# A 4 MB zero fill at the end of a kernel, changed from an SBUF store into a DRAM-to-DRAM copy with an outer dimension of 15

## The chip, the cores and the metric

The kernel runs on one core of one Trainium2 chip. The metric is the device time of one execution in microseconds, as the median of several.

## The reference

The reference computes one decode step of a small transformer block (attention over the last 4096 of 32768 cached positions, then a gated layer) and all gradients. What matters here is the size of two of the outputs: the gradients of the K cache and of the V cache.

```python
Hq, Dh = 16, 256
Hkv, Sk = k_cache.shape[1], k_cache.shape[2]          # 8, 32768
W = min(4096, max(256, Sk // 4))                      # 4096
k = jnp.repeat(k_cache[:, :, Sk - W:, :], rep, axis=1)
v = jnp.repeat(v_cache[:, :, Sk - W:, :], rep, axis=1)
...                                                   # scores, softmax, output, gated layer
_out, _vjp = jax.vjp(_f, A_x, A_k_cache, A_v_cache, A_wq, A_wo, B_w_gate, B_w_up, B_w_down)
```

Each cache gradient has 8 x 32768 x 256 bf16 elements, 128 MiB. Only the last 4096 positions of each head are not zero. So seven eighths of both outputs, 224 MiB, are zeros that somebody has to write.

## The kernel before

The zeros come from a zeroed part of SBUF (`arena`). The POOL queue writes most of them throughout the kernel. A few fills of 4 MB and 2 MB, the "late jobs", go on the SP queue behind the last computed results.

```python
ZW = 8192
def zero_rows(o, g, n0, n1, f):
    reg = o[0, g, 0:Sk - W, :].rearrange("s d -> (s d)")[n0 * 128 * ZW:n1 * 128 * ZW]
    return reg.rearrange("(n p f) -> n p f", p=128, f=f)

late_jobs = [(out_2, G - 1, 5, 7, 2 * ZW), (out_3, G - 1, 0, 6, 2 * ZW), (out_3, G - 1, 6, 7, ZW)]
...
def send_fills(n0, n1, halves=False):                  # the POOL queue
    for reg in fills[n0:n1]:
        ...
        ZQ.dma_start(out=reg, in_=zeros)
...
for it, g in enumerate(order):                         # the eight heads of the backward pass
    ...
    for o_ap, st_ in ((out_3, stV), (out_2, stK)):
        LD.dma_start(out=o_ap[0, g, Sk - W:, :].rearrange("(p t) d -> p t d", t=T), in_=st_)
    ...
for o, g, n0, n1, f in late_jobs:                      # the SP queue
    reg = zero_rows(o, g, n0, n1, f)
    for i in range(reg.shape[0]):
        LD.dma_start(out=reg[i], in_=ar(2 * ZW - f, f))
```

The last stores on the SP queue are, in this order: four of 2 MB (results), then the late fills of 4 MB, 4 MB and 2 MB. The change is about the second of the two 4 MB fills.

## Time and profile before

| what | value | from |
|---|---|---|
| time | 802.11 us (801.46 to 802.81) | three executions |
| DMA busy | 9 tenths or more in 39 of 40 slices | slices of the page |
| moved | 334.84 MB, mean 418 GB/s | slices of the page |
| last work of PE, DVE, ACT | before 720 us | windows |
| end of the slowest DMA engine | 799.0 us | packet records |

These lines are from the page of the kernel before: the span, the slices of the DMA engines, and the queues (packets, bytes, and the share of the time of 16 engines).

```profile
span 800.5 us, 8486 instructions
...
DMA  9999999999999999999999999999999999999994
GB/s 350 431 430 429 428 430 430 427 428 428 431 426 422 428 417 409 420 422 428 433 423 425 424 430 428 429 426 426 424 427 423 426 420 425 423 424 427 423 440 192
...
q0 software_dynamic: 16496, 216.01, 63.8%
q1 hardware_dynamic: 11382, 116.68, 34.7%
...
q8 instruction: 25, 0.41, 0.2%
...
HBM read 53.69 MB, written 280.59 MB: 418 GB/s over the span
```

The DMA row says that the engines are busy from start to end; q0 is the POOL queue, q1 the SP queue. So the span is bytes divided by rate, except for the last slice, whose DMA share falls to 4 tenths. The next view is the table by windows of the kernel before. Its columns are the window, its length, busy time and instructions of PE, PEld, DVE, ACT and POOL, the granted clock, the mean busy share of the 16 DMA engines, and GB/s.

```profile
720.00:740.00 20.00, 0.00 (x0) 0.00 (x0) 0.00 (x0) 0.00 (x0) 0.00 (x0) 0.50 1.03 429
...
775.00:780.00 5.00, 0.00 (x0) 0.00 (x0) 0.00 (x0) 0.00 (x0) 0.00 (x0) 0.50 0.99 426
780.00:785.00 5.00, 0.00 (x0) 0.00 (x0) 0.00 (x0) 0.00 (x0) 0.00 (x0) 0.50 0.97 416
785.00:790.00 5.00, 0.00 (x0) 0.00 (x0) 0.00 (x0) 0.00 (x0) 0.00 (x0) 0.50 0.74 315
790.00:795.00 5.00, 0.00 (x0) 0.00 (x0) 0.00 (x0) 0.00 (x0) 0.00 (x0) 0.50 0.18 75
795.00:800.50 5.50, 0.00 (x0) 0.00 (x0) 0.00 (x0) 0.00 (x0) 0.00 (x0) 0.50 0.04 18
```

No compute engine works after 720 us. The share 0.04 is below one engine in sixteen (0.0625): at the end a single DMA engine is working. The view of the waits of the SP queue says the same from the other side (columns: who waited for whom, total us, times, longest us). Line 683 is the end of the program:

```profile
SPq L683 <- DMA out_dram<-arena: 52.7, 4, 28.6
```

The chain of waits is of no help here. Its last piece is an end-of-program step of DVE at 719 us, because it does not follow the draining stores.

The packet records of the trace tell more. A record has a start, a length, a size and a queue, but no engine. In this trace 99.7% of the packets of 16 KB and more that end between 470 and 560 us have another packet's start within 6 ns of their end, so records can be chained. From 460 us on I did this with a search that also respects the order of both queues; it is a reconstruction, and where two engines run in step it could swap them. In the tail it is unambiguous. The last packets of the engine that ends last, which I call A (start us, length ns, bytes; all on the SP queue):

```
784.438  1213  32768    first of eight 32 KB packets of the second 4 MB fill
...                     one every 1210 ns
792.904  1213  32768
794.113     9      4    closes the fill
794.119   611  16384    first of eight 16 KB packets of the last 2 MB fill
...                     one every 607 ns
798.369   611  16384
798.976     9      4    closes the fill, the end
```

The trace has 2820 packets of 4 bytes and 2822 semaphore updates by DMA. The 103 transfers of the POOL queue have 1648 of these packets, 16 each, so I count one per transfer and engine.

Fourteen engines end between 786.0 and 791.5 us, one (B) at 795.3, and A at 799.0.

### The profile page before, as it was taken

Reading aid. Unit: us, or ns where it says so; the run is one execution under the profiler, and the core shown is the slowest. Engines: PE = TensorE matmul, PEld = TensorE weight load, DVE = VectorE, ACT = ScalarE, POOL = GpSimd, SP = SyncE. Lnnn points to the kernel's source line nnn. Section 1 sums busy time; section 2 is a strip of 40 time slices with the busy share of each in tenths; the row PEclk is TensorE's granted clock in tenths of the full one; section 3 lists DMA queues with packets and bytes.
Section 4 is the critical chain, followed back from the end, with each engine's and each line's share of the span. In section 5 each row is a group of like instructions: output and inputs, shape, how many; then the busy total and the mean of one; then the engine's idle time right before and its main releaser. Section 6 shows DMA issues by size and latency. Waiting matters only on the chain.

```text
span 800.5 us, 8486 instructions
## 1 busy us (share of the span) xinstructions
PE 459.3 (57%) x3182; PEld 245.9 (31%) x3182; DVE 370.2 (46%) x1176; ACT 196.3 (25%) x309; POOL 62.0 (8%) x112
## 2 busy tenths in 40 slices
PE   0459999999999994623239295845262064520000
PEld 0334554545545552312129143322021022200000
DVE  2115363472552652255770975766681187660000
ACT  0143313224133100000002054643241045340000
POOL 4000000010100110101100010000000000000000
PEclk9978999999999997555559699776557567655555
DMA  9999999999999999999999999999999999999994
GB/s 350 431 430 429 428 430 430 427 428 428 431 426 422 428 417 409 420 422 428 433 423 425 424 430 428 429 426 426 424 427 423 426 420 425 423 424 427 423 440 192
DMA packets 29359, 334.84 MB, mean 418 GB/s; under 512 B 2819, under 2 KB 5894, under 8 KB 7814
## 3 DMA queue, kind: packets, MB, share of 16 engines
q0 software_dynamic: 16496, 216.01, 63.8%
q1 hardware_dynamic: 11382, 116.68, 34.7%
q10 hardware_dynamic: 1440, 1.61, 0.6%
q8 instruction: 25, 0.41, 0.2%
q14 instruction: 16, 0.13, 0.0%
HBM read 53.69 MB, written 280.59 MB: 418 GB/s over the span
## 4 chain that ended last, share of the span: by engine, by line
PE 35%; DMA 33%; DVE 15%; ACT 4%; issue 2%; another core or an unknown queue 0%; SPq 0%; ACTq 0%; DVEq 0%
DMA out_dram<-arena 19%; PE M_ps L311 11%; PE ok_ps L315 6%; PE rows_ps L255 6%; PE tr_ps L252 4%; DMA dh_bc<-in_grad_out_dram 4%; DMA arena<-in_A_k_cache_dram 4%; ACT arena L269 2%; DMA arena<-in_A_wo_dram 2%; DVE arena L645 2%; DVE arena L454 2%; DVE arena L646 2%; DMA arena<-in_B_w_up_dram 2%; PE dqb_ps L497 2%; DMA arena<-in_B_w_gate_dram 2%; DVE arena L509 2%
## 5 line engine op out<-in xcount | busy, mean ns | idle before, releaser
L307 DVE TENSOR_SCALAR arena<-arena,p_f 128x256 bf16<-128x256 bf16 x512 | 109.8, 280 | 67.0 <-PE M_ps L311 67.0
L311 PE MATMUL M_ps<-arena 128*128 128x512 bf16 x512 | 122.9, 381 | 0.0
L255 PE MATMUL rows_ps<-arena,vpad 128*16 128x512 bf16 x256 | 85.9, 431 | 22.2 <-DVE arena L608 16.9
L252 PE MATMUL tr_ps<-ident_bf,arena 128*128 128x128 bf16 x1024 | 87.9, 236 | 15.0 <-DMA arena<-in_A_k_cache_dram 8.4
L132 POOL DMA_DIRECT2D out_dram<-arena x90 | 48.8, 544 | 560.7 <-DMA out_dram<-arena 522.7
L252 PEld LDWEIGHTS <-arena 128*128 128x128 bf16 x1024 | 65.9, 105 | 65.0 <-issue 55.4
L638 PE MATMUL d_ps<-arena,rT 32*128 32x512 bf16 x256 | 43.6, 511 | 69.6 <-DVE arena L646 50.2
L269 ACT COPY arena<-tr_ps 128x1024 bf16<-128x1024 bf16 x64 | 61.7, 1015 | 87.9 <-PE tr_ps L252 87.9
L311 PEld LDWEIGHTS <-arena 128*128 128x128 bf16 x512 | 46.2, 99 | 50.8 <-issue 6.5
L315 PE MATMUL ok_ps<-arena 128*16 128x256 bf16 x512 | 57.5, 273 | 0.9 <-DVE arena L296 0.9
L606 ACT COPY arena<-tr_ps 128x1024 bf16<-128x1024 bf16 x32 | 32.5, 1016 | 96.1 <-PE tr_ps L252 39.3
L642 ACT CAST arena<-d_ps 128x512 bf16<-128x512 f32 x64 | 37.6, 588 | 71.5 <-PE d_ps L638 71.5
L645 DVE CAST arena<-d_ps 128x512 bf16<-128x512 f32 x64 | 43.9, 686 | 14.9 <-PE d_ps L638 14.6
L315 PEld LDWEIGHTS <-arena 128*16 128x16 bf16 x512 | 45.4, 90 | 13.9 <-issue 3.4
L646 DVE CAST arena<-d_ps 128x512 bf16<-128x512 f32 x64 | 43.5, 680 | 8.3 <-DMA out_dram<-arena 8.3
L638 PEld LDWEIGHTS <-rT 32*128 32x128 bf16 x256 | 11.2, 95 | 95.4 <-issue 52.1
L643 ACT CAST arena<-d_ps 128x512 bf16<-128x512 f32 x64 | 38.0, 594 | 9.1 <-DMA out_dram<-arena 9.1
L255 PEld LDWEIGHTS <-vpad 128*16 128x16 bf16 x256 | 18.9, 91 | 57.1 <-issue 49.3
L318 ACT COPY arena<-M_ps 128x512 f32<-128x512 f32 x16 | 8.6, 589 | 75.0 <-PE M_ps L311 75.0
L509 DVE CUSTOM_DVE_ANT_0 arena<-arena 128x4096 bf16<-128x4096 bf16 x3 | 13.1, 4422 | 23.1 <-ACT arena L502 23.1
L608 DVE COPY arena<-tr_ps 128x1024 bf16<-128x1024 bf16 x32 | 21.7, 680 | 4.1 <-PE tr_ps L252 4.0
L631 DVE TENSOR_SCALAR arena<-R_sb,tl_f 128x512 bf16<-128x512 bf16 x64 | 17.8, 347 | 2.1 <-ACT R_sb L628 1.9
(198 smaller groups left out, 358.1 us busy)
## 6 DMA issues: line engine op xcount, KB each, us to landing
out_dram<-arena POOLq DMA_DIRECT2D x103, 2048.0 KB, 53.5
out_dram<-arena SPq DMA_DIRECT2D x18, 2048.0 KB, 32.7
arena<-in_A_v_cache_dram SPq DMA_DIRECT2D x10, 2048.0 KB, 49.6
arena<-in_A_k_cache_dram SPq DMA_DIRECT2D x8, 2048.0 KB, 29.7
out_dram<-arena SPq DMA_DIRECT2D x4, 4096.0 KB, 57.2
arena<-in_A_wq_dram SPq DMA_DIRECT2D x2, 3072.0 KB, 20.5
arena<-in_A_wo_dram SPq DMA_DIRECT2D x2, 1792.0 KB, 16.2
out_dram<-arena SPq DMA_DIRECT2D x2, 1792.0 KB, 33.2
```

The lines of the kernel that those rows point to most:

```text
L132: ZQ.dma_start(out=reg, in_=zeros)
L252: nc.tensor.transpose(tr_ps[:, dh, i, :], X_sb[:, 4 * q + i, dh * 128:(dh + 1) * 128], ident_bf[:])
L255: nc.tensor.matmul(rows_ps[:], lhsT=pad[:, dh, 16 * q:16 * q + 16], rhs=XT[:, dh].rearrange("p t k -> p (t k)"), start=(q == 0 and dh == 0 ...
L269: sT_ps = dots(kv_at(K_off[g]), KT_slot, vpad[g % 2], rows1, ps_c, "cols", lambda q, XT, ps: nc.scalar.copy(out=XT, in_=ps))
L307: nc.vector.tensor_scalar(out=pK[:, i, hh, :], in0=K_sb[:, t, :], scalar1=p_f[:, 8 * i + c, hh:hh + 1], scalar2=None, op0=ALU.mult)
L311: nc.tensor.matmul(M_ps[:, vh, :], lhsT=V_sb[:, t, vh * 128:(vh + 1) * 128], rhs=pK[:, i, :, :].rearrange("p h d -> p (h d)"), start=(t == ...
L315: nc.tensor.matmul(ok_ps[:, k, :], lhsT=ppad[g % 2][:, 8 * (t % 4) + t // 4, :], rhs=X_sb[:, t, :], start=(g == 0 and k == 0 and t == 0), ...
L638: nc.tensor.matmul(d_ps[:, qi].rearrange("p w d -> p (w d)"), lhsT=rT[32 * q:32 * (q + 1), :], rhs=RB_[32 * q:32 * (q + 1), l, :], start=T ...
L642: nc.scalar.copy(out=stV[:, t:t + 2, :], in_=d_ps[:, :, 0, :])
L643: nc.scalar.copy(out=stK[:, t:t + 2, :], in_=d_ps[:, :, 1, :])
L645: nc.vector.tensor_copy(out=stV[:, t:t + 2, :], in_=d_ps[:, :, 0, :])
L646: nc.vector.tensor_copy(out=stK[:, t:t + 2, :], in_=d_ps[:, :, 1, :])
```

## The change

The intent is to take one fill off the engine that ends last. The copy has an outer dimension of 15, to leave one of the sixteen engines out; if that one is the late one, it is spared 9.7 us. The source is a region of the K gradient that was zeroed hundreds of microseconds earlier.

```diff
+        done = zero_rows(out_2, 0, 0, 2, 2 * ZW)[0].rearrange("p f -> (p f)")
+
+        def fifteen(flat):
+            return flat[0:15 * 17 * ZW].rearrange("(a b) -> a b", b=17 * ZW)
+
         for o, g, n0, n1, f in late_jobs:
             reg = zero_rows(o, g, n0, n1, f)
             for i in range(reg.shape[0]):
-                LD.dma_start(out=reg[i], in_=ar(2 * ZW - f, f))
+                if (n0, i) == (0, 2):
+                    with tc.issue_after(getattr(last, "ins", last)):
+                        flat = reg[i].rearrange("p f -> (p f)")
+                        for lo, hi in ((0, 16 * ZW), (16 * ZW, 17 * ZW)):
+                            LD.dma_start(out=fifteen(flat)[:, lo:hi], in_=fifteen(done)[:, lo:hi])
+                        LD.dma_start(out=flat[255 * ZW:256 * ZW].rearrange("(o f) -> o f", o=1), in_=done[255 * ZW:256 * ZW].rearrange("(o f) -> o f", o=1))
+                else:
+                    last = LD.dma_start(out=reg[i], in_=ar(2 * ZW - f, f))
```

The three copies are 15 x 4 x 64 KB, 15 x 16 KB and 16 x 1 KB. Nothing else moves on any engine.

## The prediction

The packet records carry no engine numbers. A number in this text is a place in an order that the mapping runs below give: engine n carries a packet of every tiny SP-queue copy of more than n rows, and of none with n rows or fewer. Engine 15 is then the one that a copy of 15 rows leaves out.

> **What bounds the kernel.** DMA. The page's slices show the 16 DMA engines at 9 tenths or more in 39 of 40 slices; 334.84 MB went at a mean of 418 GB/s. Compute ends by about 720 us of the 800.5 us span (the table by windows shows PE, DVE and ACT at 0.00 after that). From there only queued stores drain, so the kernel ends when the slowest DMA engine has emptied its queue.
>
> **The tail is uneven.** By windows the DMA share is 0.97 in 780 to 785 us, 0.74 in 785 to 790, 0.18 in 790 to 795 and 0.04 in 795 to 800.5. In the packet records of the trace the last packets form separate back-to-back chains, one per engine (16 KB every 607 ns, 32 KB every 1210 ns): fourteen engines finish between about 786 and 791.5 us, one (call it B) at 795.3, one (A) at 799.0. A is alone for 3.7 us. A's delay was already 9.4 us against the median landing of every late store from 746 us on. The 16 KB instruction-fetch packets (25, about 0.93 us each) probably caused it by sitting on one engine; that is an inference, since the records do not number engines.
>
> **What the change does.** The second-to-last store (4 MB, arena to output, eight 32 KB packets per engine, 9.7 us per engine) becomes three DMAs from the zeroed cache output: 15 x 4 x 64 KB, 15 x 16 KB, and 16 x 1 KB. Order on PE, DVE, ACT and POOL is unchanged; SP issues two more DMAs, long before the queue reaches them. [...] So the intent is to relieve A, if A is engine 15; this trace cannot show that.
>
> **The sum.** The spared engine loses 9.7 us. The other fifteen get 272 KB instead of 256 KB: 17 x 607 ns = 10.3 us, +0.6 us, plus about 0.06 us for the 1 KB piece, if a DRAM-to-DRAM packet costs what SBUF-to-DRAM does (no packet of this trace shows one; the cache loads, DRAM to SBUF, do run at the same 611 ns per 16 KB). If A is spared: A ends at about 789.4, B at 795.3 + 0.7 = 796.0, and B becomes the last. Gain 799.0 - 796.0 = 3.0 us: 802.1 becomes 799.1. If A is not spared: +0.7 us. Each 10% by which DRAM-to-DRAM is slower per byte costs B 1.0 us; at 1.3 times the gain is gone, at twice the time is about 806.
>
> **Prediction** 799.5 us, 796.8 to 806.0. Faster by over 2%: 0.01, within 2%: 0.95, slower by over 2%: 0.04.
>
> **What would show it.** The windows of the last 20 us: the lone 0.04 stretch gone or shortened, the share in 785 to 795 up. Read bytes up by 4.2 MB. In the packet records, new 64 KB packets of about 2.43 us; longer ones mean DRAM-to-DRAM is slower.
>
> **What would make it wrong.** A is not engine 15 (I give 0.35); reading and writing the same memory at once slows the fifteen engines (0.3); a read of the output waits for other writes to that output.

The sum comes to 799.0 - 796.0 = 3.0 us of gain if A is spared, 802.1 - 3.0 = 799.1 us, and to 0.7 us of loss if it is not. Why engine 15 would be spared, and why it would be a late one: the trace of before shows neither, so the 0.65 that the forecast gave to this step is its author's estimate. The 0.06 us for the 1 KB piece is an estimate too; the 448 packets of 1 KB on the SP queue in that trace took 46 to 52 ns.

## The result, and the profile after

The changed kernel took 802.90 us (802.80 to 803.39, four executions) against 801.81 us (801.46 to 802.81, four) of the kernel before. The ratio is 1.0013, with a 95% interval of 0.9995 to 1.003: the same within 2%, and no gain.

From the page of the changed kernel, the lines that answer to those of before:

```profile
span 801.3 us, 8465 instructions
...
GB/s 349 429 429 430 429 430 429 429 430 428 430 427 418 428 418 409 421 421 426 434 424 426 420 429 428 428 426 427 425 425 424 425 420 424 425 422 428 424 417 203
...
HBM read 57.89 MB, written 280.59 MB: 422 GB/s over the span
```

4.2 MB more are read, as planned. The last two slices changed from 440 and 192 to 417 and 203 GB/s. The windows of the changed kernel:

```profile
775.00:780.00 5.00, 0.00 (x0) 0.00 (x0) 0.00 (x0) 0.00 (x0) 0.00 (x0) 0.50 0.93 364
780.00:785.00 5.00, 0.00 (x0) 0.00 (x0) 0.00 (x0) 0.00 (x0) 0.00 (x0) 0.50 0.91 364
785.00:790.00 5.00, 0.00 (x0) 0.00 (x0) 0.00 (x0) 0.00 (x0) 0.00 (x0) 0.50 0.81 337
790.00:795.00 5.00, 0.00 (x0) 0.00 (x0) 0.00 (x0) 0.00 (x0) 0.00 (x0) 0.50 0.39 164
795.00:801.00 6.00, 0.00 (x0) 0.00 (x0) 0.00 (x0) 0.00 (x0) 0.00 (x0) 0.50 0.06 27
```

Two things stand out. At 775 to 780 us the share is 0.93 where it was 0.99 before, and at 780 to 785 us 0.91 where it was 0.97: one engine, a sixteenth, is missing. And the last stretch still has the share of about one engine. So an engine was taken out, but not the one that ends last. The issue of the copies is not the reason: the timeline of the SP queue (start us, duration us, what) has them issued between 744.7 and 756.1 us, and A reaches them at 784.6 us.

```profile
744.65 2.44 SPq L667 DMA_DIRECT2D out_dram<-out_dram  x2
755.50 0.57 SPq L668 DMA_DIRECT2D out_dram<-out_dram  x1
760.36 0.34 SPq L670 DMA_DIRECT2D out_dram<-arena  x1
```

The packet records settle it for this execution. The engine that ends last, at 799.8 us, carries the copy. The engine that carries no 64 KB packet ends at 777.2 us:

```
last engine, changed kernel (start us, length ns, bytes)
781.753  1349  32768    the last two packets of the first 4 MB fill, slower than 1213
783.099  1465  32768
784.566  2458  65536    the copy: 2458, 2432, 2436, 2422
...
791.881  2422  65536
794.306   611  16384    its second part
794.919    46   1024    its third part
794.967   611  16384    first of eight of the last 2 MB fill
...
799.831     9      4    the end

spared engine: 32768 x8, 1024 x1, 16384 x8, end at 777.165 us
```

Before, A needed 784.438 to 794.113 us for its share of this fill, 9.68 us. Now it needs 784.566 to 794.967 us, 10.40 us. That is 0.72 us more, because each of fifteen engines gets 273 KB instead of 256 KB. A further 0.13 us was there before its copy began.

### The profile page after: what moved, and what is told of

Read it like the earlier page. It is cut to its first block, busy times and chain, and to the rows that moved or that the text cites. A ratio compares the mean times of both kernels' runs of the same rounds, so it can differ in the third digit from the quotient of the medians.

```text
span 801.3 us, 8465 instructions
## 1 busy us (share of the span) xinstructions
PE 458.5 (57%) x3159; PEld 247.2 (31%) x3182; DVE 370.3 (46%) x1176; ACT 196.3 (25%) x309; POOL 61.8 (8%) x112
## 4 chain that ended last, share of the span: by engine, by line
PE 36%; DMA 33%; DVE 15%; ACT 4%; issue 2%; another core or an unknown queue 0%; SPq 0%; DVEq 0%; ACTq 0%
DMA out_dram<-arena 19%; PE M_ps L311 11%; PE ok_ps L315 6%; PE rows_ps L255 6%; DMA arena<-in_B_w_gate_dram 5%; PE tr_ps L252 5%; DMA dh_bc<-in_grad_out_dram 4%; DMA arena<-in_A_k_cache_dram 4%; ACT arena L269 2%; DVE arena L645 2%; DVE arena L454 2%; DVE arena L646 2%; PE dqb_ps L497 2%; DVE arena L423 2%; DVE arena L509 1%
## 5 line engine op out<-in xcount | busy, mean ns | idle before, releaser
L311 PE MATMUL M_ps<-arena 128*128 128x512 bf16 x489 | 120.5, 381 | 1.5 <-issue 0.4
```

The source lines that it names most:

```text
L311: nc.tensor.matmul(M_ps[:, vh, :], lhsT=V_sb[:, t, vh * 128:(vh + 1) * 128], rhs=pK[:, i, :, :].rearrange("p h d -> p (h d)"), start=(t == ...
```

## The experiments

Theory 1 is that the late engine A is not the one left out, engine 15, and was not spared. Theory 2 is that A was spared, and that copying inside DRAM on fifteen engines at once ate the gain. A second question is why A is late at all. All twelve kernels gave correct results.

### Which engine is late: `map_even` and `map_odd`

Tiny copies of k rows were put between the last large stores on the SP queue, each k with its own packet size. If the engines of a smaller copy are always among those of a larger one, the set of tiny packets on a chain tells its engine's place in that order, its number in this text. The traces show whether they are.

```diff
+        def probe(q, k, n):                # k rows of n elements
+            return q.dma_start(out=rows_of(spot, k, n), in_=rows_of(src, k, n))
 ...
+                        for k in ...:      # even run 4, 8, 12 and 2, 6, 10; odd run 5, 9, 13 and 3, 7, 11
+                            probe(LD, k, 640 + 32 * k)
```

> The kernel before with six tiny copies of 2, 4, 6, 8, 10 and 12 rows put between the last large stores on the SP queue, each with its own packet size, and three tiny copies of 15 rows on the POOL queue. [...] the engine that finishes last (A) tells its number, to within two, by which of the six packets it carries. Theory 1 (the fifteen-engine copy did not spare A): A carries at least one of them, so its number is below 12, or none and it is 12 to 14. Theory 2 (A is engine 15 and was spared, the gain was eaten elsewhere): A carries none of the six. The POOL copies show which engine a 15-row copy on that queue leaves out. The time is not the object: about 803 us, up to 2 us more.

> The changed kernel with six tiny copies of 3, 5, 7, 9, 11 and 13 rows between the last large stores. With the even run this gives each late engine's number exactly; the engine without 64 KB packets is the spared one. Theory 1: the spared engine carries none of the tiny packets (it is engine 15 or 14) and ends some 12 us before the others, and A carries 64 KB packets. Theory 2: the spared engine is the one that ended last before. Time about 803 to 805 us.

Both ran as single executions (803.15 and 803.74 us). In the even run A ended at 799.7 us and carried the packets of 6, 8, 10 and 12 rows, not those of 2 and 4: it is engine 4 or 5. In the odd run A ended at 800.4 us and carried 5, 7, 9, 11 and 13, not 3, and it carried 64 KB packets: it is engine 3 or 4. So A is engine 4, if it is the same engine in both runs. In the odd run the engine without 64 KB packets carried the 16-row piece of 1 KB and none of the six tiny packets. It is not among the first 13 engines and not among the first 15, so it is engine 15. On each chain named here and under `probe_sw` the copies are all those from some number of rows up: from 6 in the even run, from 5 in the odd run, from 2, 4, 5 and 7 in `probe_sw`. So far the sets are nested, and the numbers mean no more than this order. The even run also had three copies of 15 rows on the POOL queue; which engine they leave out was not worked out.

### The copy without the sparing, and the sparing without the copy: `copy16` and `sbuf15`

```diff
 copy16
-                        (three copies, outer dimension 15)
+                        LD.dma_start(out=flat.rearrange("(a b) -> a b", b=16 * ZW), in_=done.rearrange("(a b) -> a b", b=16 * ZW))
 sbuf15
-                        (three copies, outer dimension 15)
+                        c = 120 * 2 * ZW
+                        LD.dma_start(out=flat[0:c].rearrange("(p f) -> p f", p=120), in_=ar(0, 2 * ZW)[0:120])
+                        LD.dma_start(out=flat[c:c + 120 * 1024].rearrange("(p f) -> p f", p=120), in_=ar(0, 1024)[0:120])
+                        LD.dma_start(out=flat[255 * ZW:256 * ZW].rearrange("(p f) -> p f", p=16), in_=ar(0, 512)[0:16])
```

> The 4 MB fill as a DRAM-to-DRAM copy on all sixteen engines (64 rows of 64 KB), nothing spared. Theory 1 (A is not spared, and comes to its copy after most engines have finished theirs, so it copies at full rate): A has the same bytes as before, time as before within 1 us, ratio 0.999 to 1.002, against 1.0013 of the change. Theory 2 (A was spared, the DRAM-to-DRAM rate ate 3 us): without sparing, A pays as well, ratio at least 1.004.

> The 4 MB fill from the arena on fifteen engines (120 partitions of 32 KB, 120 of 2 KB, 16 of 1 KB): the sparing without the DRAM-to-DRAM copy. Theory 1: A carries its fifteenth, 17/16 of the bytes: before plus about 0.7 us, ratio 1.000 to 1.002. Theory 2: A is spared and nothing is eaten: 3 us less than before, ratio 0.996.

`copy16` took 802.41 us against 802.27 us, ratio 1.0003 (0.9989 to 1.0016). So copying inside DRAM costs the kernel nothing that these rounds can show. Not that the copies run at full rate: a 64 KB packet took 2418 ns at the least (four times 604 ns), but 2726 ns in the mean of its 64 packets, and 2649 ns in the mean of the changed kernel's 60. The 32 KB stores from 768 us on took 1308 ns in the mean in the changed kernel, against 1217 in the kernel before. But A comes last, when most of the others are done, and in the changed kernel its four packets took 2422 to 2458 ns. Theory 2 needed at least 1.004 and falls.

`sbuf15` was a miss of both theories: 812.33 us, ratio 1.0134 (1.012 to 1.0149), 10 us slower. Its windows:

```profile
775.00:780.00 5.00, 0.00 (x0) 0.00 (x0) 0.00 (x0) 0.00 (x0) 0.00 (x0) 0.50 1.08 311
780.00:785.00 5.00, 0.00 (x0) 0.00 (x0) 0.00 (x0) 0.00 (x0) 0.00 (x0) 0.50 0.88 253
785.00:790.00 5.00, 0.00 (x0) 0.00 (x0) 0.00 (x0) 0.00 (x0) 0.00 (x0) 0.50 0.88 215
790.00:795.00 5.00, 0.00 (x0) 0.00 (x0) 0.00 (x0) 0.00 (x0) 0.00 (x0) 0.50 0.77 229
```

The engines are busy, 0.88 of them, but move less: 253 and 215 GB/s, where a share of 0.91 moved 364 in the changed kernel. The 32 KB packets after 768 us have a mean of 1698 ns and a maximum of 4995 ns, against a mean of 1225 ns from 700 to 768 us. The page has 2849 packets under 512 B against 2819 before. That is 30 more, as many as the changed kernel has more packets of 4 bytes (1105 against 1075 on the SP queue): 15 + 15 + 16 in place of 16, so this fill went to fifteen engines as well. Why the packets are slower was not shown. What the run does show is that this SBUF form of a fifteen-engine fill costs 10 us, while with the DRAM form of the change the median rose by 1.1 us.

### Does engine 4 alone set the end: `rows4`, `rows5` and `shift4`

An extra copy of 4 or of 5 rows of 64 KB was put ahead of the last 2 MB fill. The two kernels differ by one packet on engine 4.

```diff
                 if n0 == 6:
+                        last = LD.dma_start(out=rows_of(4, K, 32768), in_=rows_of(0, K, 32768))   # K = 4 or 5
                         LD.dma_start(out=reg[i], in_=ar(2 * ZW - f, f))
```

> The kernel before plus one extra DRAM-to-DRAM copy of 4 rows of 64 KB (zeros onto zeros) ahead of the last 2 MB fill: engines 0 to 3 get 2.42 us more each, engine 4 nothing. Theory 1 (engine 4 alone sets the end; the others have 3 us or more of room): no change, ratio 0.999 to 1.001. Rival (the end is set by the bytes on all engines, or by one of engines 0 to 3): 0.2 us for 256 KB spread over all, or +2.4 us, ratio 1.003, if the last engine is one of 0 to 3.

> The same with 5 rows of 64 KB: engine 4 gets one too. Theory 1: engine 4's end and the kernel move by one 64 KB packet, +2.42 us, ratio 1.003, while rows4 does not move. If engine 4 were not the last: the same as rows4.

`rows4` took 802.21 us against 802.39 us, ratio 0.9998 (0.9984 to 1.0012). `rows5` took 804.69 us, ratio 1.0025 (1.0012 to 1.0038). So 256 KB more on engines 0 to 3 cost nothing that these rounds can show, and 64 KB more on engine 4 cost 2.3 us by the medians, close to the 2.42 us of its packet. This is the most direct evidence: for the time it needs no chains of packets, only the order of the mapping runs, in which A carried the copy of 5 rows and not that of 4. The traces add a limit. In that of `rows5` the chain that ends last, at 801.6 us, carries a 64 KB packet, and the next one ends at 799.5. In that of `rows4` (an execution of 802.96 us, the second longest of five) the chain that ends last, at 799.8 us, also carries a 64 KB packet, so it is one of engines 0 to 3, and the latest chain without one ends at 798.7. In that execution the extra packet had used up the room.

`shift4` tried to make use of it. It moves 384 KB of the fill from all engines to engines 0 to 3.

```diff
-                        (the 4 MB fill, 128 rows of 32 KB)
+                        LD.dma_start(out=flat[0:CUT].rearrange("(p f) -> p f", p=128), in_=ar(0, 14848))
+                        for lo in (0, PART):      # two copies of 4 rows of 48 KB
+                            LD.dma_start(out=four(flat, lo), in_=four(done, lo))
```

> The kernel before with 384 KB of the 4 MB fill taken from all sixteen engines (29 KB rows for 32 KB rows) and copied by engines 0 to 3 instead, in two copies of 4 rows of 48 KB: engine 4 has 24 KB less, 0.9 us; engines 0 to 3 have 72 KB more, 2.7 us. Theory 1: engine 4 ends 0.9 us earlier, at about 798.1, and one of engines 0 to 3, if it is the one that ended at 795.3, at 798.0: 0.9 us less, ratio 0.9989, better than both kernels by a little. Rival: no gain, or a loss where engines 2 or 3 become the last.

It took 802.53 us against 802.39 us, ratio 0.9998 (0.9986 to 1.0011): no gain. In its trace the chain without 48 KB packets that ends latest does so at 798.2 us, 0.7 us earlier than A in the trace of before. But a chain with them, so one of engines 0 to 3, ends at 799.4 us and is the new last one. The room of engines 0 to 3 was smaller than the single trace of before suggested, as the trace of `rows4` shows too.

### Can a small transfer be put on the upper engines: `probe_sw`

```diff
+        for how, k, n in ((0, 8, 1400), (0, 8, 1432), (1, 8, 1464), (1, 8, 1496), (0, 4, 1528), (0, 4, 1560), (0, 3, 1592)):
+            from_sbuf(k, n) if how else probe(ZQ, k, n)       # the POOL queue
```

> The kernel before with tiny copies of 4, 5, 6 and 2, 3, 7 rows between the last large stores on the SP queue, and seven tiny transfers of 8, 8, 8, 8, 4, 4 and 3 rows on the POOL queue after its last fill. The two mapping runs point to engine 4 as the last engine, 2 and 6 as the next. If that is right, the last chain carries the packets of the 5-, 6- and 7-row copies and none of 2, 3 and 4; the next two carry those of 3 to 7 rows, and of 7 rows alone. The POOL transfers ask whether a transfer of fewer than 16 rows can be put on the upper engines (which would allow sparing engine 4): if the sets move from transfer to transfer, no engine has the packets of both 8-row copies; if they are always the lowest engines, the same engines have all of them. About 803 to 805 us.

A single execution, 803.28 us. A ended at 799.8 us and carried the packets of 5, 6 and 7 rows and none of 2, 3 and 4: engine 4 again, in one run. The next ones were not as expected; a chain ending at 798.1 us carried all six packets (engine 0 or 1), one at 797.5 only that of 7 rows (engine 6), one at 797.1 those of 4 to 7 rows (engine 3). So only A's place was the same in these runs. On the POOL queue, the packets of the four 8-row transfers follow each other on each of eight engines 0.2 to 0.5 us apart; none moved on to the other eight. So I found no way to spare engine 4 and not those above it, and no version that beats both kernels.

### Why is engine 4 late: `pe_extra`, `pe_extra2`, `dve_extra` and `dve_extra2`

The prediction guessed that A carries the instruction fetches of PE. In the trace of before, q8 has 25 packets of 16 KB, which took 878 to 965 ns each, and from one to the next 126 matmuls start in the mean. 3182 matmuls and 3182 weight loads on 25 packets are 255 instructions each, so I count 256 to a fetch (estimate). The test adds tiny matmuls on PE after its last work, when nothing waits for it. The control does it on VectorE.

```diff
+        spin_ps = ps_t.tile([128, 16], f32, tag="tmp", name="spin_ps")
+        with tc.issue_after(getattr(pe_last, "ins", pe_last)):
+            for n in range(512):                       # pe_extra2: 1280
+                nc.tensor.matmul(spin_ps[:], lhsT=ident_bf[:], rhs=ident_bf[:, 0:16], start=True, stop=True)
 the control
+        spin = lnw.tile([128, 16], f32, name="spin")
+        with tc.issue_after(getattr(dve_last, "ins", dve_last)):
+            for n in range(1024):                      # dve_extra2: 256
+                nc.vector.memset(spin[:], 0.0)
```

> The kernel before with 512 tiny matmuls (1024 instructions, four instruction fetches of 16 KB) on the idle PE after its last work at about 720 us; they end before 775 us and nothing waits for them. Theory F (A is late because it carries PE's instruction fetches): four more fetches on A, each 0.6 to 1.3 us, so A's end and the kernel move by 2.4 to 5.2 us, ratio 1.003 to 1.0065. Rival R (A is late because its path or port is slower, whatever is fetched): no change, ratio 1.000 within 0.001.

> The control of pe_extra: the kernel before with 1024 tiny memsets on the idle VectorE after its last work[...]. Theory F with DVE's fetches on the second-last engine B, which has 3.7 us of room: [...] B moves by 2.4 to 5.2 us, the kernel by 0 to 1.5 us. If DVE's fetches were on A: the kernel moves by 2.4 to 5.2 us. Rival R: no change.

The size and the number of VectorE's instruction fetches no trace here shows; the 2.4 to 5.2 us for them rest on these alone and are the author's estimate.

`pe_extra` took 804.73 us against 802.32 us, ratio 1.003 (1.0017 to 1.0042), as theory F had it. `dve_extra` was a failed experiment: its memsets took 145 us and ended at 867 us, so VectorE itself set the time, 869.94 us. From its timeline:

```profile
722.15 145.00 DVE L663 MEMSET spin<- 128x16 f32 x1024
```

The trace of `pe_extra` contradicted the theory that had just predicted the time. Its four new fetches lie on four different chains, and none of them is A. What A has instead are fourteen POOL-queue packets of 16 KB that took 100 to 170 ns longer than 611 ns, all while the added matmuls ran. In the kernel before, after 715 us, there is no such packet. So there were two more runs.

> 1280 tiny matmuls after PE's last work instead of 512: they run from about 720 to about 782 us, ten instruction fetches instead of four. In pe_extra the four fetches lay on four engines other than engine 4, and fourteen 16 KB packets of POOL's queue took 100 to 170 ns longer than 611 ns while the matmuls ran, which the kernel before does not have. Theory F (each PE fetch costs engine 4 about 0.6 us): +6 us, ratio 1.0075. Theory Q (busy PE issue slows only packets of POOL's queue on engine 4; that queue is empty by 748 us): +2.4 us as with 512, ratio 1.003. Rival: the 2.4 us of pe_extra were an accident of that build: ratio 1.000.

> The VectorE control with 256 memsets, so that VectorE ends at about 758 us, well before the stores (1024 memsets ended at 867 us and set the time themselves). [...] If the late engine is slowed by any engine's dense tiny instructions: +1 to 2 us; if by PE alone: no change, ratio 0.999 to 1.001.

`pe_extra2` took 808.26 us against 802.13 us, ratio 1.0075 (1.0062 to 1.0089). `dve_extra2` took 802.90 us, ratio 1.001 (0.9997 to 1.0023), not clear of zero: the control leaves open whether VectorE's instructions do the same. The view by source line of `pe_extra2` shows the added instructions, on line 663 (columns: engine and operation, xcount, min/median/max ns, first and last start us). They end at 789 us, before the stores do in any kernel here.

```profile
L663 PEld LDWEIGHTS <-ident_bf x1280: 103/104/119, 719.7 to 789.3; 128*128 128x128 bf16 x183
L663 PE MATMUL spin_ps<-ident_bf x1280: 174/174/196, 719.7 to 789.3; 128*128 128x16 bf16 x183
```

The timeline of PE in the same kernel has three of the bursts (start us, duration us, what, and in brackets the idle time before and what it ended by):

```profile
758.73 3.58 PE L663 MATMUL spin_ps<-ident_bf 128*128 128x16 bf16 x128 [3.71 <-issue]
766.02 3.58 PE L663 MATMUL spin_ps<-ident_bf 128*128 128x16 bf16 x128 [3.71 <-issue]
773.32 3.58 PE L663 MATMUL spin_ps<-ident_bf 128*128 128x16 bf16 x128 [3.71 <-issue]
```

The matmuls come in bursts of 128, the contents of one fetch, for 3.6 us, with 3.7 us of waiting for the next; q8 has 35 packets here, ten more than before. From 758.73 us the bursts start every 7.3 us. The slow packets of A come in the same bursts: at 759.1 to 761.3 us, at 766.4 to 768.6, at 773.6 to 775.8, now on the SP queue as well, so theory Q falls too. The fetch before the first of these bursts lasts from 756.5 to 757.4 us. The slow packets go with the execution of the instructions, or with its recording, and not with their fetch.

I then took, for each reconstructed chain, the packets of 8 KB and more, and fitted the length above the usual one to the number of instructions of each engine that started while the packet was under way (kernel before, from 461 us):

```
chain ending at   ns per PE or PEld instr.   per DVE      per ACT
798.985 (A)            1.7 +- 0.1           2.6 +- 0.5   7.7 +- 0.6
795.283 (B)           -0.2 +- 0.1           1.9 +- 0.8   0.2 +- 1.0
791.448                0.1 +- 0.2          -0.5 +- 0.9   1.8 +- 1.2
788.934               -0.1 +- 0.1          -0.2 +- 0.4   0.0 +- 0.5
```

All other chains have PE values between -0.3 and 0.1. In `pe_extra2` A has 2.0 +- 0.1 and the other fifteen between -0.1 and 0.1. These fits are only as good as the chains. A second, simpler chaining again gave A alone a high value in `pe_extra2` (1.7 +- 0.2). In the kernel before it either found none or, from 641 us on, one chain with 1.6 +- 0.2 that did not end as A. So the value of A in the kernel before is argued, not shown. The experiments give a figure of the same size without any chaining: 6.1 us for 2560 added instructions is 2.4 ns each, and 2.4 us for 1024 is 2.4 ns each. If the fitted values hold, an estimate from them, 6405 recorded PE and PEld starts at 1.7 ns, 1373 DVE at 2.6 and 431 ACT at 7.7, gives 18 us of extra work on engine 4 in a whole run. A ends 9.3 us after the median of the chains and 13 us after the earliest; in the fit the other engines have more of other small delays (3 to 9 ns per packet against 1 ns of A), which may account for the difference (not shown).

What engine 4 does in this time stays open. If it moves bytes at the rate of the packets, 16384 bytes in 607 ns, 2.4 ns are about 64 bytes per PE instruction (an estimate; that it moves any was not shown). As every execution here was recorded, no run shows whether engine 4 is late in a kernel that nobody records.

## Why the prediction was right or wrong

The measured 802.9 us lies inside the range of 796.8 to 806.0 us, and "within 2%" was right. The central value, 799.5 us, and its reason were not. The range held both outcomes, since the prediction's own "not spared" gives 802.1 + 0.7 = 802.8 us, so lying inside it says nothing for the mechanism.

- That DMA bounds the kernel and that the end is the slowest engine's end: right. `rows4` and `rows5` show it by one packet on engine 4, with the limit told there.
- The step that failed: "So the intent is to relieve A, if A is engine 15", taken at 0.65. A is engine 4: so say the even and the odd run taken together, and `probe_sw` by itself. The spared engine 15 ended at 777.2 us, and its gain was worth nothing. The step rested on reasons that the trace of before does not show, and the runs contradict it for this kernel.
- "If A is not spared: +0.7 us": right. A needed 10.40 us in place of 9.68 us, 0.72 us more; the span grew by 0.8 us, the median by 1.1 us.
- "+0.6 us ... if a DRAM-to-DRAM packet costs what SBUF-to-DRAM does": right for A, 2422 to 2458 ns for 64 KB against the 2430 ns assumed. Wrong for the crowd, 2649 ns in the mean, 9% more. That was harmless, as those engines have room.
- A read of the output waiting for other writes: did not matter. Waits of 9.9 and 8.4 us for earlier stores stood before the copies on the SP queue (in the kernel before, 13.0 us in three before its late fills), but the first copy was issued at 744.7 us, 40 us ahead of its use by A.
- "The 16 KB instruction-fetch packets ... probably caused it by sitting on one engine": wrong. In `pe_extra` they lie on four engines other than A. The link to PE's instructions held in the runs that added some, the carrier did not.

## What to carry to other kernels

When a kernel ends with one DMA engine working alone, find out which engine that is before sparing one: tiny copies of k rows with distinct packet sizes, between the last stores, gave its place in one run or two here, because the engines of a smaller copy were among those of a larger one. A transfer with fewer than 16 rows spared only the upper engines here (2 to 13 rows in the tiny copies, 15 in the change), so it can relieve engine 15 and not engine 4. And when a change adds work to many engines, only what it adds to the last one counts, until another has used up its room: 64 KB more on engine 4 cost 2.3 us, and 256 KB on engines 0 to 3 nothing that the rounds of `rows4` can show, but in its trace one of these ended last.
